# Linear attention and its feed-forward on one core: a fourth r/k slot in the decoder's scratch, r*k on another engine, and a new order

## The chip, the cores and the metric

The kernel runs on one core of one Trainium2 chip. The time is device microseconds of that core, from launch to the last instruction. A time is the median of several runs; beside them stands one profiled execution, from which every trace row here comes. PE is TensorE, DVE VectorE, ACT ScalarE, POOL GpSimd, SP the engine whose queue issues the transfers.

## The reference

Inputs are r, k, v, w of shape (4, 8, 768, 48), u of (8, 48), and two weights of (384, 2048) and (2048, 384), all float32.

```python
def _attn_ref(r, k, v, w, u):
    for t in range(S):                                   # S = 768
        cur = einsum('bhd,bhe->bhde', u[None] * k[t], v[t])
        y[t] = einsum('bhd,bhde->bhe', r[t], state + cur)
        state = w[t][..., None] * state + einsum('bhd,bhe->bhde', k[t], v[t])
    return y

def _moe_ref(x, w_in, w_out):                            # x: y as (3072, 384)
    h = x @ w_in
    g = where(h >= 1, h, where(h <= -1, 0, (h + 1)**2 / 4))
    return g @ w_out
```

## The kernel before

**Two stages in one program.** Attention goes in 12 units `u` of 256 tokens, three per batch entry. The feed-forward goes in 6 blocks `b` of 512 tokens, each made of two units, and in 16 slices `f` of the hidden width. Every feed-forward product is made of three products in a rounded format (high by high, high by low, low by high), so one step is 9 matmuls into `h` (L960) and 9 into `acc` (L980), with a gate between them: ACT L763, L764, DVE L765, ACT L767, DVE L768. Blocks 0 and 1 begin with half-width steps (`HALVES`, 5 and 11 of them for each half), so that a block can begin when its first unit is there. `h` has two PSUM banks, `g`, `gh` and `gl` three buffers each.

**A unit.** For each of two halves `q` (1 first) SP loads a `wq` tile and an `rk` tile (r and k side by side). DVE makes two scans (L439 forward, L434 backward), multiplies k (L468) and r (L518) by them; PE makes products among tokens (L488), transposes (L527), state updates (L549) and the outputs (L598); DVE picks the lower triangle (L494) and adds the states (L567 to L570). The term with u is made in two ways. In units 0 to 3 (`EARLY`) it is a scaled copy `ku` and one more set of L488. From unit 4 on a tile `nk` with r and k in another layout is loaded; POOL multiplies its halves (L506), DVE multiplies by u (L508) and sums (L511), POOL spreads the sums over `r` (L514), and DVE and PE go on. At the end ACT and DVE write `x` and `last` (L653, L655), and six small transfers (L700) fill the rest of `x`.

**Slots.** `wq` and `rk` have three slots each; a unit takes `(2u + 1 - q) % 3` of both, so one of the two tiles of the next unit waits until this unit's last matmul has read its slot.

**Weights.** They come as 64-bit words, 768 KB for each f (`wraw`, L351), at most three in flight. ACT L360 and L363, POOL L364, DVE L366, ACT L356 and DVE L369 turn them into the high and the low weight. Two scratch tiles `fl` and one `rr` hold what is between. After the decode, `fl` serves as room for 12 loads of w that a later check (L719, L720) reads.

**Unit 0** has v and a small permutation `perm` loaded in padded form (L423, L424): v into `g0` and `g1`, `perm` into a part of `nk`.

**The start of PE.** `warm` (L322) issues `SMALL` products of zeros and clears the eight banks; later, where the plan expects PE to idle for over 0.5 us, `zeros` (L335) puts products of zeros (L331) into the gap.

**The order.** Nothing is ordered by hand. `Plan.add` takes each operation with an engine, a cost, what it reads and writes, and a due time; `Plan.order` (L133) is a list scheduler that walks through modelled time and lets each free engine take, of the operations that are ready, that with the smallest key. The key is the planned time of the step that needs it, less a lead: `LEADS[u]` or `DECODES[f]` plus `SLACK` times the cost of the chain still behind it, for loads `LOADS` or `RAWS` besides. `products` into `acc` get `-LAG * AFTER` as lead, so a larger `AFTER` puts them behind other PE work. `port=True` marks operations for which DVE and POOL are modelled as sharing one port. The order that comes out is what each engine's in-order queue gets.

Of the kernel before, what the change touches and what calls it, by code (L numbers as in the profile page):

```python
# [8 lines left out]
F32 = mybir.dt.float32  # L9
# [15 lines left out]
C = 64  # L25
NC = UT // C
SEG = 2 * (UT + 1)
HP = 64
# [12 lines left out]
SMALL = 48  # L41
# [7 lines left out]
class Plan:  # L49
# [19 lines left out]
    def add(self, engine, cost, emit, due, reads=(), writes=(), port=False, size=0, fresh=True, mode=128, spare=0.0):  # L69
# [9 lines left out]
        for x in writes:  # L79
# [3 lines left out]
                             fresh=fresh and engine == "PE", touch={*reads, *writes}, mode=mode, spare=spare))  # L83
# [49 lines left out]
    def order(self):  # L133
# [10 lines left out]
        open_ = {e: [] for e in ("PE", "SP", "ACT", "DVE", "POOL")}  # L144
# [15 lines left out]
        while any(open_.values()):  # L160
# [24 lines left out]
            if op["port"]:  # L185
                port = free[e]
                first.clear()
# [31 lines left out]
SLACK = 0.759  # L219
LEADS = {0: 384.81, 1: 606.87, 2: 40.05, 3: 27.03, 4: 45.45, 5: 71.8, 6: 60.98, 7: 25.74, 8: 81.18, 9: 211.42, 10: 77.25, 11: 123.12}  # L220
DECODES = [100.35, 69.7, 39.12, 146.42, 32.88, 6.81, -6.35, -7.47, 249.78, -36.61, 27.78, -83.98, 25.56, 23.26, -16.63, -161.0]
LOADS = {0: 9.57, 1: -384.0, 2: -5.47, 3: 9.66, 4: 7.78, 5: -12.47, 6: 37.12, 7: 0.0, 8: 6.52, 9: -48.34, 10: -46.8, 11: -16.85}
RAWS = [0.0, -4.85, -25.68, 4.86, 33.83, -3.4, -2.07, 2.55, -2.88, 0.0, 79.29, 0.0, 0.0, 5.35, 18.51, -22.93]
FLIGHT = 3

EARLY = 4

GUARDED = 6

# [6 lines left out]
STEP, FIRST, PACED, AFTER = 27.1568, 703.402, 25.4941, 8.52  # L236
# [3 lines left out]
def attention_moe(tc, a):  # L240
# [46 lines left out]
    fl = tiles(2, [128, 768], F32, "fl")  # L287
    rr = one([128, 768], I32, "rr")
# [25 lines left out]
    op("POOL", 0.5, SOON, (), [("g", 2), ("s", "g2")], lambda: G.memset(g_[2][:, 0:256], 0.0))  # L314
    wide_st = {"ob0": ob[:, 0:256], "ob1": ob[:, 256:512], "g2": g_[2][:, 0:256]}
# [6 lines left out]
    def warm():  # L322
        for n in range(SMALL):
            g, h = n // 2 % 2, n % 2
            PE.matmul(bank[h][HP * g : HP * g + C, 0:C], lhsT=zero[HP * h : HP * h + HP, 0:C], rhs=zero[HP * h : HP * h + HP, 0:C],
                      start=True, stop=True)
        for b in bank:
            cleared(b, 4)
# [3 lines left out]

    op("PE", 0.16 + 0.054 * SMALL + 0.43 * 8, SOON, ["zero", "clear"], [("b", i) for i in range(8)], warm)

# [8 lines left out]
    def weight(f, when):  # L343
# [13 lines left out]

        op("SP", 0.45, due, (), [("raw", f), ("flight", f % FLIGHT)], fetch, size=786432)

# [690 lines left out]
```

## Time and profile before

| | |
|---|---|
| median of 3 runs | 505.94 us (504.72 to 509.08) |
| profiled execution | 508.8 us, its span 507.1 us |
| instructions | 13246 |
| bytes moved | 54.12 MB, mean 107 GB/s |
| HBM read, written | 46.32 MB, 4.72 MB |
| granted TensorE clock, mean | 0.998 |
| ACT busy | 296.1 us (58%) |
| POOL busy | 100.4 us (20%) |

Times in the rows further down are counted from the span's start, 1.7 us less than the device time in all. In the table of lines a group gives instructions, total, and mean; a matmul's duration reaches from its start to a modelled end and overlaps with the next, so PE's pace is read from where groups start. Products of zeros count as busy.

### The profile page before, as it was taken

Reading aid. Unit: us, or ns where it says so; the run is one execution under the profiler, and the core shown is the slowest. Engines: PE = TensorE matmul, PEld = TensorE weight load, DVE = VectorE, ACT = ScalarE, POOL = GpSimd, SP = SyncE. Lnnn points to the kernel's source line nnn. Section 1 sums busy time; section 2 is a strip of 40 time slices with the busy share of each in tenths; the row PEclk is TensorE's granted clock in tenths of the full one; section 3 lists DMA queues with packets and bytes.
Section 4 is the critical chain, followed back from the end, with each engine's and each line's share of the span. In section 5 each row is a group of like instructions: output and inputs, shape, how many; then the busy total and the mean of one; then the engine's idle time right before and its main releaser. Section 6 shows DMA issues by size and latency. Waiting matters only on the chain.

```text
span 507.1 us, 13246 instructions
## 1 busy us (share of the span) xinstructions
PE 492.8 (97%) x5562; PEld 412.5 (81%) x5562; DVE 332.2 (66%) x560; ACT 296.1 (58%) x605; POOL 100.4 (20%) x68
## 2 busy tenths in 40 slices
PE   8999999999999999999999899999999999999995
PEld 6778987889999988888878678888887888888884
DVE  6899997956998699849555979842364333243331
ACT  3597798987875564745643565653454444454441
POOL 2487766801012321102001112100010000000000
PEclk9999999999999999999999999999999999999999
DMA  8984734326643434505006342300110000100001
GB/s 297 403 296 147 281 145 153 126 64 208 201 126 97 140 108 143 167 11 204 23 1 193 106 134 90 123 1 1 63 49 13 17 1 0 63 2 0 1 1 67
DMA packets 21922, 54.12 MB, mean 107 GB/s; under 512 B 3104, under 2 KB 8672, under 8 KB 21856
## 3 DMA queue, kind: packets, MB, share of 16 engines
q1 hardware_dynamic: 21856, 53.21, 31.5%
q8 instruction: 45, 0.74, 0.6%
q14 instruction: 21, 0.17, 0.1%
HBM read 46.32 MB, written 4.72 MB: 101 GB/s over the span
## 4 chain that ended last, share of the span: by engine, by line
PE 75%; DVE 13%; DMA 4%; ACT 3%; issue 3%; SPq 1%; ACTq 0%; DVEq 0%
PE h L960 33%; PE acc L980 33%; PE bank L598 4%; DVE y L434 2%; DVE gl L768 2%; PE bank L488 2%; DMA rk<-in_rk 2%; DVE p L439 1%; DMA wraw<-in_wbits 1%; DVE wt L369 1%; PE bank L527 1%; PE bank L549 1%; DVE r L494 1%; DMA wq<-in_w 1%; DVE g L765 1%
## 5 line engine op out<-in xcount | busy, mean ns | idle before, releaser
L960 PE MATMUL h<-x,wt 128*128 128x512 f32 (+1 forms) x1008 | 216.8, 361 | 1.9 <-DVE g L765 1.3
L960 PEld LDWEIGHTS h<-x,wt 128*128 128x128 f32 x1008 | 168.3, 188 | 31.8 <-DVE g L765 1.9
L980 PE MATMUL acc<-gh,wt 128*128 128x512 f32 (+1 forms) x672 | 152.2, 360 | 0.0
L980 PEld LDWEIGHTS acc<-gh,wt 128*128 128x128 f32 x672 | 113.8, 188 | 19.0
L765 DVE SCALAR_TENSOR_TENSOR g<-g,h 128x512 f32<-128x512 f32 (+1 forms) x112 | 67.4, 605 | 92.1 <-ACT g L764 84.9
L763 ACT ACTIVATE g<-h 128x512 f32<-128x512 f32 (+1 forms) x112 | 59.7, 533 | 85.8 <-PE h L960 84.1
L768 DVE TENSOR_TENSOR gl<-g,gh 128x512 fp32r<-128x512 f32 (+1 forms) x112 | 73.3, 659 | 28.9 <-ACT gh L767 13.5
L767 ACT CAST gh<-g 128x512 fp32r<-128x512 f32 (+1 forms) x112 | 62.1, 558 | 39.6 <-PE acc L980 18.6
L980 PE MATMUL acc<-gl,wt 128*128 128x512 f32 (+1 forms) x336 | 84.5, 357 | 0.1
L980 PEld LDWEIGHTS acc<-gl,wt 128*128 128x128 f32 x336 | 58.4, 187 | 10.0 <-DVE gl L768 0.5
L764 ACT ACTIVATE g<-g 128x512 f32<-128x512 f32 (+1 forms) x112 | 64.0, 571 | 3.3
L364 POOL TENSOR_SCALAR rr<-wraw 128x768 uint16<-128x768 f32 x16 | 52.7, 3291 | 35.0 <-DVE fl L366 17.3
L514 POOL TENSOR_TENSOR r<-cst,d 128x512 f32<-128x512 f32 x16 | 17.3, 1104 | 157.0 <-PE bank L598 131.9
L506 POOL TENSOR_TENSOR nk<-nk 128x768 f32<-128x768 f32 x8 | 16.8, 2096 | 83.7 <-DMA nk<-in_nk 74.5
L439 DVE TENSOR_TENSOR_SCAN p<-wq,seeds 128x514 f32<-128x514 f32 x24 | 30.2, 1259 | 3.7 <-DMA wq<-in_w 2.8
L434 DVE TENSOR_TENSOR_SCAN y<-wq,seeds 128x514 f32<-128x514 f32 x24 | 30.8, 1282 | 0.8
L468 DVE TENSOR_TENSOR rk<-rk,y 128x512 f32<-128x512 f32 x24 | 18.9, 789 | 3.1 <-DMA rk<-in_rk 2.9
L331 PE MATMUL bank<-clear 128*128 128x512 f32 (+1 forms) x57 | 17.1, 418 | 1.8 <-DVE seeds L438 1.8
L369 DVE TENSOR_TENSOR wt<-fl,wt 128x768 fp32r<-128x768 f32 x16 | 16.5, 1033 | 3.2 <-ACT wt L356 3.1
L598 PEld LDWEIGHTS bank<-rk,st 48*48 48x48 f32 (+1 forms) x656 | 11.4, 121 | 8.6 <-DVE st L567 2.9
L363 ACT ACTIVATE rr<-wraw 128x768 uint16<-128x768 uint32 x16 | 17.5, 1094 | 1.1 <-DVE fl L366 1.1
L518 DVE TENSOR_TENSOR rk<-rk,p 128x512 f32<-128x512 f32 x24 | 17.7, 749 | 0.2 <-PE acc L488 0.2
(108 smaller groups left out, 384.5 us busy)
## 6 DMA issues: line engine op xcount, KB each, us to landing
rk<-in_rk SPq DMA_DIRECT2D x24, 512.0 KB, 4.8
wraw<-in_wbits SPq DMA_DIRECT2D x16, 768.0 KB, 7.9
wq<-in_w SPq DMA_DIRECT2D x24, 257.5 KB, 3.3
nk<-in_nk SPq DMA_DIRECT2D x8, 768.0 KB, 4.8
vn<-in_v SPq DMA_DIRECT2D x11, 384.0 KB, 5.8
fl<-in_w SPq DMA_DIRECT2D x12, 257.0 KB, 2.9
out_y<-g SPq DMA_DIRECT2D x11, 256.0 KB, 2.3
x<-last SPq DMA_DIRECT2D x66, 32.0 KB, 2.5
```

Of the source, the lines that this page charges most:

```text
L364: op("POOL", 3.35, due, [("raw", f)], ["rr_high"], lambda: G.tensor_scalar(out=r16[:, :, 1], in0=wraw[f][:, :, 1].bitcast(F32), scalar1=0. ...
L369: op("DVE", 0.95, due, [("fl", k), ("wh", f)], [("wl", f)], lambda: V.tensor_tensor(out=w_lo[f], in0=s, in1=w_hi[f].bitcast(F32), op=ALU.s ...
L434: V.tensor_tensor_scan(out=y_[:, ::-1], data0=w[:, SEG:0:-1], data1=sv[:, ::-1], initial=0.0, op0=ALU.mult, op1=ALU.add)
L439: V.tensor_tensor_scan(out=pv[:, q].rearrange("p n c -> p (n c)"), data0=w[:, 0:SEG], data1=sv, initial=0.0, op0=ALU.mult, op1=ALU.add,)
L598: PE.matmul(out=bank[by[g]][HP * half : HP * half + wide, lo : lo + C], start=first, stop=False, skip_group_check=True, **kw)
L763: op("ACT", c, due, [("b", 6 + hk)], [("g", gk)], lambda: nc.scalar.activation(gs, hs, AF.Relu, scale=0.5, bias=0.5))
L764: op("ACT", c, due, (), [("g", gk)], lambda: nc.scalar.activation(gs, gs, AF.Square))
L765: op("DVE", 0.13 + 0.56 * k, due, [("b", 6 + hk)], [("g", gk)], lambda: nc.vector.scalar_tensor_tensor(out=gs, in0=gs, scalar=1.0, in1=hs, ...
L767: op("ACT", c, due, [("g", gk)], [("gh", gk)], lambda: nc.scalar.copy(ghs, gs))
L768: op("DVE", 0.18 + 0.52 * k, due, [("g", gk), ("gh", gk)], [("gl", gk)], lambda: nc.vector.tensor_tensor(out=gls, in0=gs, in1=ghs.bitcast( ...
L960: nc.tensor.matmul(by16(hp, f), lhsT=wx[f][:, cs], rhs=by16(xt[:, j, :], f), start=n == 0, stop=n == 8)
L980: nc.tensor.matmul(by16(o[j]), lhsT=wx[f][:, cs], rhs=by16(gt), start=first and i == 0, stop=stop and i == 2, skip_group_check=True)
```

## The change

- `fl`, `rr` and three new uses share one tile `scratch`: two `fl` and `rr` as before, then, when all weights are decoded, a fourth slot of `rk` (columns 0 to 1023) and two `stage` tiles (1024 to 1535 and 1536 to 2047).
- From unit 4 on (`FOUR`) a unit takes the slots `u % 2` and `u % 2 + 2` of `rk`; `wq` keeps three. Loads into slot 3 wait for all 16 decodes.
- Block outputs with j = 1 and 2 go out through `stage`, no longer through `g1` and `g2` (except in the last block), and the check's loads of w go to `stage`, without the column that isn't needed.
- r*k in `nk` (L506) moves from POOL to DVE.
- Unit 0 takes v as the other units do and ACT spreads it into `g0` and `g1`, cleared by POOL; `perm` is made on POOL from the identity. Three loads become one.
- `warm` makes 12 products of 256 columns where it made 48 of 64.
- The plan: new leads, `SLACK` 2.283 for 0.759, `AFTER` 122.415 for 8.52; loads are planned to land 1 us later than before (`MARGIN`); POOL's L364, L450 and L514 now stand in the model as holding the port for 0.8, 0.27 and 0.93 us.

```diff
-SMALL = 48
+SMALL = 12
...
             if op["port"]:
-                port = free[e]
+                port = free[e] if op["hold"] is None else t + op["hold"]
...
-SLACK = 0.759
-LEADS = {0: 384.81, 1: 606.87, 2: 40.05, 3: 27.03, 4: 45.45, 5: 71.8, 6: 60.98, 7: 25.74, 8: 81.18, 9: 211.42, 10: 77.25, 11: 123.12}
-DECODES = [100.35, 69.7, 39.12, 146.42, 32.88, 6.81, -6.35, -7.47, 249.78, -36.61, 27.78, -83.98, 25.56, 23.26, -16.63, -161.0]
+SLACK = 2.283
+LEADS = {0: 313.28, 1: 332.14, 2: 30.3, 3: -35.92, 4: 59.61, 5: 8.14, 6: 58.69, 7: -189.33, 8: -17.53, 9: 10.22, 10: -177.85, 11: 56.6}
+DECODES = [151.83, 107.97, 105.43, 231.96, 14.9, -48.19, 3.2, 263.77, 168.2, 7.46, 92.06, 298.21, 156.44, 134.24, 312.98, 121.85]
...
+MARGIN = 1.0
+FOUR = 4
...
-STEP, FIRST, PACED, AFTER = 27.1568, 703.402, 25.4941, 8.52
+STEP, FIRST, PACED, AFTER = 27.1568, 703.402, 25.4941, 122.415
...
-    fl = tiles(2, [128, 768], F32, "fl")
-    rr = one([128, 768], I32, "rr")
+    scratch = one([128, 3 * 768], F32, "scratch")
+    fl = [scratch[:, 0:768], scratch[:, 768:1536]]
+    rr = scratch[:, 1536:2304].bitcast(I32)
+    rk = [*rk, scratch[:, 0:1024].rearrange("p (a c) -> p a c", a=2)]
+    stage = [scratch[:, 1024:1536], scratch[:, 1536:2048]]
+    decoded = [("wl", f) for f in range(NF)]
...
-            PE.matmul(bank[h][HP * g : HP * g + C, 0:C], lhsT=zero[HP * h : HP * h + HP, 0:C], rhs=zero[HP * h : HP * h + HP, 0:C],
-                      start=True, stop=True)
+            PE.matmul(bank[h][HP * g : HP * g + C, 0 : 4 * C], lhsT=zero[HP * h : HP * h + HP, 0:C],
+                      rhs=zero[HP * h : HP * h + HP, 0:C].unsqueeze(1).broadcast_to([HP, 4, C]), start=True, stop=True)
...
-        slot = [(2 * u + 1 - q) % 3 for q in range(2)]
+        wslot = [(2 * u + 1 - q) % 3 for q in range(2)]
+        slot = wslot if u < FOUR else [u % 2, u % 2 + 2]
+        behind = [] if u < FOUR else decoded
...
+            load(due, rk[slot[q]], a["rk"][u, q], [("k", slot[q]), ("r", slot[q])], behind if slot[q] == 3 else [], spare=MARGIN if u > 1 else 0.0)
...
         if alone:
+            load(due, v[:, :, 0:DM], a["v"][u], [("v", 0)])
             for c2 in range(2):
-                load(due, g_[c2], a["v0"][c2], [("g", c2)])
-            load(due, perm, a["perm"], ["perm", "nk"])
+                op("ACT", 0.48, due, [("v", 0)], [("g", c2)], lambda c2=c2: A.copy(
+                    g_[c2].rearrange("p (h e) -> p h e", e=HP)[:, :, 0:D], v[:, c2, 0:DM].rearrange("p (h e) -> p h e", e=D)))
+            op("POOL", 0.4, due, (), ["perm", "nk"], lambda: G.memset(perm, 0.0))
+            op("POOL", 0.3, due, ["cst"], ["perm"], lambda: G.tensor_copy(
...
-            op("POOL", 2.2, due, (), ["nk"], lambda: G.tensor_tensor(
+            op("DVE", 0.94, due, (), ["nk"], lambda: V.tensor_tensor(
                 out=nk[:, :, 0, :], in0=nk[:, :, 0, :], in1=nk[:, :, 1, :], op=ALU.mult), port=True)
...
-            o, ok = (ob, "ob") if j == 0 else (g_[m], ("g", m))
+            o, ok = (ob, "ob") if j == 0 else (g_[m], ("g", m)) if done else (stage[j - 1], ("stage", j - 1))
```

## Rows read from the trace of the kernel before

**Rows 1.** The page: busy time, share, instructions; then tenths in 40 slices.
```profile
PE 492.8 (97%) x5562; PEld 412.5 (81%) x5562; DVE 332.2 (66%) x560; ACT 296.1 (58%) x605; POOL 100.4 (20%) x68
...
PE   8999999999999999999999899999999999999995
PEld 6778987889999988888878678888887888888884
DVE  6899997956998699849555979842364333243331
```

**Rows 2.** Busy time by stage: window, length, engines' busy us, granted clock, DMA share, GB/s.
```profile
9.50:27.50 18.00, 16.58 (x363) 13.12 (x361) 14.94 (x25) 10.11 (x21) 7.62 (x3) 1.00 1.03 405
27.50:57.30 29.80, 27.89 (x588) 24.50 (x586) 29.43 (x48) 24.00 (x51) 24.56 (x11) 1.00 0.62 208
57.30:84.00 26.70, 25.50 (x215) 22.07 (x219) 26.25 (x42) 24.51 (x42) 16.48 (x6) 1.00 0.49 187
...
118.00:300.00 182.00, 179.40 (x2385) 154.00 (x2379) 142.06 (x254) 109.46 (x258) 27.13 (x19) 1.00 0.39 124
```

**Rows 3.** The same windows, zeros alone (L331): PE busy, PEld busy, clock, DMA, GB/s.
```profile
9.50:27.50 18.00, 8.74 (x32) 5.22 (x31) 1.00 1.03 405
27.50:57.30 29.80, 4.29 (x16) 2.46 (x15) 1.00 0.62 208
57.30:84.00 26.70, 0.00 (x0) 0.00 (x0) 1.00 0.49 187
```

**Rows 4.** Waits of PE from 118 to 300 us: engine, line, releaser, total, times, longest.
```profile
PE bank L488 <- DVE seeds L438: 1.3, 1, 1.3
PE h L960 <- DVE g L765: 0.5, 1, 0.5
PE bank L598 <- DVE st L567: 0.5, 1, 0.5
```

**Rows 5.** Timeline 275 to 293 us: start, length, instruction, idle before and releaser.
```profile
276.19 0.69 DVE L468 TENSOR_TENSOR rk<-rk,y 128x512 f32<-128x512 f32 x1 [2.16 <-DMA rk<-in_rk]
...
279.19 2.03 POOL L506 TENSOR_TENSOR nk<-nk 128x768 f32<-128x768 f32 x1 [9.31 <-DMA nk<-in_nk]
279.47 2.30 DVE L518 TENSOR_TENSOR rk<-rk,p 128x512 f32<-128x512 f32 x1
...
281.82 1.16 PE L488 MATMUL bank<-rk 64*64 64x64 f32 x64 [1.28 <-DVE seeds L438]
...
292.13 0.67 PE L598 MATMUL bank<-rk,st 48*48 48x64 f32 x32 [0.53 <-DVE st L567]
```

**Rows 6.** Timeline 150 to 160 us, the same columns.
```profile
155.31 2.42 DVE L768 TENSOR_TENSOR gl<-g,gh 128x256 fp32r<-128x256 f32 x2
155.60 1.85 POOL L506 TENSOR_TENSOR nk<-nk 128x768 f32<-128x768 f32 x1 [2.57 <-DMA nk<-in_nk]
...
158.73 1.33 PE L960 MATMUL h<-x,wt 128*128 128x256 f32 x9 [0.55 <-DVE g L765]
```

**Rows 7.** Single lines: count, duration ns min/median/max, first and last start, form.
```profile
L506 POOL TENSOR_TENSOR nk<-nk x8: 1834/1853/2812, 123.7 to 307.8; 128x768 f32<-128x768 f32 x8
L508 DVE TENSOR_TENSOR nk<-nk,u_sb x8: 932/949/957, 136.7 to 312.4; 128x768 f32<-128x768 f32 x8
L518 DVE TENSOR_TENSOR rk<-rk,p x24: 665/684/2299, 11.3 to 380.0; 128x512 f32<-128x512 f32 x24
L364 POOL TENSOR_SCALAR rr<-wraw x16: 3069/3168/4090, 17.1 to 99.4; 128x768 uint16<-128x768 f32 x16
L434 DVE TENSOR_TENSOR_SCAN y<-wq,seeds x24: 1227/1228/1950, 5.4 to 329.9; 128x514 f32<-128x514 f32 x24
```

**Rows 8.** POOL's and SP's waits for `nk` and slots; landing of `nk`, issue to landing.
```profile
POOL nk L506 <- DMA nk<-in_nk: 74.5, 7, 21.2
...
SPq L301 <- PE bank L598: 105.4, 13, 24.4
...
DMA to landing us min/median/max: 4.1/4.7/6.3
```

**Rows 9.** DVE's timeline in unit 0's chain, 11 to 28 us.
```profile
12.25 1.23 DVE L439 TENSOR_TENSOR_SCAN p<-wq,seeds 128x514 f32<-128x514 f32 x1 [0.30 <-DMA wq<-in_w]
...
14.86 0.67 DVE L518 TENSOR_TENSOR rk<-rk,p 128x512 f32<-128x512 f32 x1
...
25.00 0.96 DVE L366 SCALAR_TENSOR_TENSOR fl<-fl,rr 128x768 int32<-128x768 int32 x1 [1.33 <-POOL rr L364]
```

**Rows 10.** PE's timeline: the small zeros, and the end of PE's first wait.
```profile
2.94 2.84 PE L325 MATMUL bank<-zero 64*64 64x64 f32 x96
...
9.49 0.60 PE L527 MATMUL bank<-cst,rk 128*128 128x128 f32 x4
```

## What was predicted

> **What bounds the kernel now.** I read the page first, then the windows by stage, then what ended PE's idle time, then the timelines around those places. The page says that PE is busy for 97% of the span and that no other engine comes near [rows 1]. That figure counts products of zeros, so the windows have to be read with the zeros beside them. From 9.5 to 84 us PE lost three pieces: length less busy time plus zeros is 18.00 - 16.58 + 8.74 = 10.2 us, then 29.80 - 27.89 + 4.29 = 6.2 us, then 26.70 - 25.50 = 1.2 us, together 17.6 us [rows 2, 3]. In the same three windows DVE was idle for only 3.06 + 0.37 + 0.45 = 3.9 us of 74.5. So this stage, in which four units of attention and sixteen weight decodes meet, belongs to DVE. From 118 to 300 us PE lost 182.00 - 179.40 = 2.6 us, and 2.3 us of them are three waits for DVE [rows 2, 4]. There DVE itself has 182.00 - 142.06 = 39.9 us free. After that the tenths of PE stand at 9 to the last slice [rows 1]: a pure PE stage, whose work the change leaves alone.
>
> So there are two places to win in: 2.3 us in the middle, up to 17.6 us in the start. The matmuls of the two layers and of attention are the same before and after.
>
> **The change part by part.** The sum is made against the profiled execution, 508.8 us, of which 507.1 are span and 1.7 lie around it; the median of the runs is 505.94, 2.9 us lower, and a gain is taken to be the same on both.
>
> *r*k on DVE.* It removes eight POOL instructions of 1.85 us and adds eight on DVE; the nearest row is L508, same tile and shape, 0.95 us, so 8 x 0.95 = 7.6 us of DVE in a stage that has 39.9 free [rows 2, 7]. What it gives back is larger than the step itself. At 279.19 L506 runs on POOL, and a DVE product with two SBUF inputs that began 0.28 us later took 2.30 us where the line's median is 0.68; PE then waited 1.28 us [rows 5, 7]. At 155.60 the same happens: two L768 take 2.42 us together, and PE waits 0.55 us [rows 6]. The sum of these two waits is 1.8 us, and both go with L506. Bounds: nothing, if POOL's other product in that stage (L514) falls on the same DVE work instead, and the whole 2.3 us. I take 1.8.
>
> The Trainium skill, SBUF — State Buffer, section "SBUF: two separate sides", says that DVE and GpSimd share one pair of ports under an exclusive lock that the first to start keeps for its whole instruction. The 1.6 us by which L518 grew agree with it. By the same rule the moved product can itself be held up by L514, which stays on POOL, and each L364 would hold such DVE work for its 3.2 us; the longest backward scan, at 1.95 us against 1.23, shows only 0.72 us added [rows 7], so for L364 the measurement decides. By that rule taken whole, the moved product would keep some of the collisions and the 1.8 would shrink towards nothing; by the rows it stays.
>
> *The wait that moves with it.* POOL spent 74.5 us waiting for `nk` to land, at no cost, because nothing urgent stood behind [rows 8]. Now that wait stands in DVE's in-order queue, and behind it are the gates (L765, L768) that PE needs. The transfer takes 4.7 us from issue to landing and 6.3 at worst, a spread of 1.6 us [rows 8]. The plan has 1 us of margin on it, and PE carries up to two steps of `acc` products as cover. I price it at nothing; without the cover it is up to 1.6 us in each of 8 units, 12.8 us. It is the rival on the slower side.
>
> *The fourth slot.* SP waited 13 times and 105.4 us in all for the matmul that frees a slot [rows 8]. In one place this reached PE: L468 waited 2.16 us for `rk` at 276.19, DVE then had three scans and the triangles in a heap, and PE waited another 0.53 us at 292.13 [rows 5]. With four slots a unit's tiles can be loaded a whole unit earlier. This gives 0.5 us, bounds 0 and 0.5 beside the term above. Slots 3 and `stage` are aliases of decode scratch; every use comes after the last decode, and the last L364 starts at 99.4 us [rows 7], before unit 5 needs a slot. Outputs through `stage` take the out-transfers off `g1` and `g2`; no row of PE's waits shows such a stall [rows 4], so nothing.
>
> *Twelve wide zeros.* The same columns in a quarter of the instructions. The 48 took 2.84 us from 2.94 us on, and PE's first real work comes at 9.49 us [rows 10], after more zeros. Hidden by that wait, either way. The granted clock is 1.00 in the windows from 9.5 us on [rows 2], and nothing says that the wide ones keep PE less busy. Nothing.
>
> *Unit 0 without three loads, and the new order, taken together.* Both act on the stage of 9.5 to 84 us. `v` and `perm` are 320 KB less in all; at the 405 GB/s of that window [rows 2] the first weights land 0.8 us earlier, and two copies of about half a microsecond go to an ACT that is idle for 7.9 of 18 us. The order: unit 0's second L518 (14.86) stands behind a scan pair of unit 1 that began at 12.25 [rows 9], so its chain could be 2.6 us shorter. Bounds: at best PE gets back the 6.2 + 1.2 us of the later windows and 2.6 + 0.8 of the first, 10.8 us. At worst the order puts a unit's four scans (4 x 1.23 = 4.9 us) in front of something that PE waits for. The nearest row for a middle value is DVE's own idle time: if the same DVE work has to be done in this stage, 3.9 us is all that can be won, and about 0.9 of it are gaps of a hop that no order closes. I take 3.0. What speaks for a gain at all: the decodes get leads of mostly over 100 us, the products into `acc` become PE's last choice and so a reserve, and unit 3, whose output is needed only in block 1's second half, gets a lead of -36 us in place of 27.
>
> Sum: 1.8 + 0.5 + 3.0 = 5.3 us; 508.8 - 5.3 = 503.5 as a profiled execution, 505.94 - 5.3 = 500.6 us as a median.
>
> **The rivals.** *The start stays as it is.* DVE is busy for 95% of 9.5 to 84 us whatever the order, and a weight's decode passes five times between engines. Then only the middle is won: 505.94 - 2.3 = 503.6 us. For it speaks that the DVE work of the stage is unchanged; against it that PE's lost 17.6 us are over four times DVE's idle 3.9, so part of it is choice.
>
> *The change does not reach PE.* The new loads are asked for no earlier than before, since the plan places them by due times, and the moved product meets L514 instead of L506. Then it is 505.9 us. For it: PE idled for 2.6 of 182 us in the middle anyway. Against: the two stalls lie exactly under L506.
>
> *DVE stands in line for `nk`.* One mechanism: the moved product waits at the head of DVE's queue. Place: units 4 to 11. Price: up to 1.6 us uncovered in each. It decides when the units lose more on average than the 5.3 us won plus 5.1 (1%), that is 10.4 / 8 = 1.3 us each, which needs PE's reserve of `acc` products to be empty each time. At that point the time is 511 us, at full price 505.94 - 5.3 + 12.8 = 513.4 us.
>
> **How the numbers follow.** A measurement of this kernel can tell about 1% (5 us) from no change. My forecast, the gain in both places, has 0.46: around 500.6, its own range 495.6 to 503 (the lower end is 505.94 - 2.3 - 8, most of the 10.8). The start unchanged has 0.32, no reach 0.10, the wait for `nk` or another misordering with more cost than gain 0.12. Faster by over 1% is below 500.9 us, where I put the larger part of the forecast and of luck in the start: 0.46. Within 1%: 0.41, from the second and third case and the upper part of the first. Slower by over 1%: 0.13. The range leaves out most of the slower case and the best end of the start: 495.5 to 508.5, where 508.5 is 505.94 + 4.9 - 2.3.
>
> **What would show it.** In the trace after: no POOL instruction of `nk` and no DVE product of two SBUF inputs above 1 us outside L514 and L364; PE's waits between 118 and 300 us below 1 us in all; the first L960 before 27 us; zeros from 9.5 to 57 us below 13.0 us; PE's waits naming neither `nk` nor the new product. The forecast is wrong if zeros and idle time before 84 us stay near 17 us, if L768 or L765 wait for the DMA of `nk`, or if PE goes idle at the start of a block.

## The result and the profile after

The changed kernel takes 501.59 us (median of 4 runs, 500.79 to 503.27); the kernel before, on the same chip, took 506.16 (4 runs, 504.72 to 509.08). The ratio is 0.9896, with a 95% interval of 0.9867 to 0.9926: 4.6 us gained where 5.3 were forecast. A second set of runs (after_again below) gives 0.9866 and 6.9 us, so the forecast lies between the two. Its profiled execution took 503.27 us, of which 501.6 are span. The lines have moved: zeros L331 is L341, the weight's decode L364, L366 and L369 is L374, L376 and L379, the scans L434 and L439 are L451 and L456, the two loads' products L468 and L518 are L485 and L535, r*k L506 is L523, L488 is L505, L598 is L615, the gates L765 and L768 are L782 and L785, and the feed-forward products L960 and L980 are L977 and L997.

The page's busy times answer [rows 1]. r*k's eight products have left POOL, which is busy for 16.5 us less; DVE has eight instructions more and is nevertheless busy for 5.2 us less.

```profile
PE 491.2 (98%) x5488; PEld 412.4 (82%) x5488; DVE 327.0 (65%) x568; ACT 298.1 (59%) x607; POOL 83.9 (17%) x64
```

The stages of [rows 2], the same columns: window, length, busy time and count of PE, PEld, DVE, ACT and POOL, granted clock, DMA share, GB/s.

```profile
9.50:27.50 18.00, 15.30 (x342) 12.67 (x332) 12.87 (x22) 9.08 (x19) 7.96 (x3) 0.91 0.99 376
27.50:57.30 29.80, 29.03 (x580) 25.50 (x582) 28.02 (x49) 24.83 (x53) 21.43 (x11) 1.00 0.56 201
57.30:84.00 26.70, 26.70 (x367) 23.59 (x360) 25.74 (x44) 26.11 (x51) 18.25 (x8) 1.00 0.57 213
118.00:300.00 182.00, 182.00 (x2553) 157.04 (x2552) 147.06 (x278) 103.39 (x243) 16.20 (x14) 1.00 0.36 116
```

The zeros alone (L341) in the first two, as in [rows 3]; the third window again has none.

```profile
9.50:27.50 18.00, 7.53 (x26) 5.04 (x27) 0.91 0.99 376
27.50:57.30 29.80, 6.76 (x24) 3.55 (x22) 1.00 0.56 201
```

The middle is as forecast: from 118 to 300 us PE idles for 0 us, where it was 2.6. The start is not: length less busy time plus zeros is 10.2 + 7.5 + 0 = 17.8 us, against 17.6 before. PE's timeline also has the first feed-forward product later, at 31.18 us; before it came at 27.46. The kernel before, then the changed one:

```profile
27.46 1.22 PE L960 MATMUL h<-x,wt 128*128 128x256 f32 x6
...
31.18 2.04 PE L977 MATMUL h<-x,wt 128*128 128x256 f32 x15
```

Yet the start did give something, and counting PE's matmuls shows it. First the kernel before from 0 to 84 and 84 to 300 us, all engines, then L960, L980, L331 and the outputs L598 alone up to 84 us (PE and PEld):

```profile
0.00:84.00 84.00, 77.68 (x1275) 65.90 (x1279) 76.27 (x122) 62.20 (x120) 51.65 (x38) 1.00 0.69 250
84.00:300.00 216.00, 213.40 (x2705) 181.91 (x2702) 163.65 (x284) 137.98 (x308) 41.75 (x25) 1.00 0.39 122
...
0.00:84.00 84.00, 21.64 (x126) 17.88 (x126) 1.00 0.69 250
...
0.00:84.00 84.00, 18.89 (x117) 16.30 (x117) 1.00 0.69 250
...
0.00:84.00 84.00, 18.03 (x62) 11.10 (x62) 1.00 0.69 250
...
0.00:84.00 84.00, 4.79 (x248) 4.24 (x252) 1.00 0.69 250
```

Then the changed kernel, in a second profiled execution (the first experiment below): the same two stretches, then L977, L997, L341 and the outputs L615 up to 84 us.

```profile
0.00:84.00 84.00, 78.59 (x1321) 66.00 (x1321) 74.16 (x124) 63.82 (x129) 52.87 (x44) 1.00 0.70 254
84.00:300.00 216.00, 216.00 (x2827) 185.42 (x2826) 180.95 (x326) 128.27 (x285) 29.34 (x19) 1.00 0.36 118
...
0.00:84.00 84.00, 23.67 (x135) 19.40 (x135) 1.00 0.70 254
...
0.00:84.00 84.00, 16.22 (x108) 14.55 (x108) 1.00 0.70 254
...
0.00:84.00 84.00, 18.19 (x60) 11.05 (x60) 1.00 0.70 254
...
0.00:84.00 84.00, 7.12 (x368) 6.13 (x368) 1.00 0.70 254
```

At 84 us both have done 243 feed-forward products (126 + 117 and 135 + 108). Of the rest, the kernel before had 1275 - 243 - 62 - 96 (its small zeros) = 874 matmuls of attention, the changed one 1321 - 243 - 60 - 24 = 994. So 120 more matmuls of attention lie behind it at the same moment, in nearly the same "lost" time (16.9 us in this second execution). All 120 are outputs, 368 - 248, and take 7.12 - 4.79 = 2.3 us. What stands after 84 us agrees in size: 507.1 - 84 = 423.1 us before, 500.8 - 84 = 416.8 after, 6.3 less. Of these, 2.6 are the idle time removed; 0.5 are a shorter end behind PE's last matmul, which ends at 501.74 us before and at 495.91 after; the other 3.2 are work already done at 84 us. The "lost" time does not show this gain, and since a matmul's end is modelled, PE's busy time does not price it.

### The profile page after: what moved, and what is told of

Same layout as the page of the kernel before. It is cut to its first block, busy times and chain, and to the rows that moved or that the text cites. A ratio compares the mean times of both kernels' runs of the same rounds, so it can differ in the third digit from the quotient of the medians.

```text
span 501.6 us, 13003 instructions
## 1 busy us (share of the span) xinstructions
PE 491.2 (98%) x5488; PEld 412.4 (82%) x5488; DVE 327.0 (65%) x568; ACT 298.1 (59%) x607; POOL 83.9 (17%) x64
## 4 chain that ended last, share of the span: by engine, by line
PE 91%; DVE 2%; issue 0%; ACT 0%; ACTq 0%; DVEq 0%
PE acc L997 40%; PE h L977 40%; PE bank L615 5%; PE bank L505 3%; PE bank L544 2%; PE bank L566 2%; DVE r L511 0%; DVE scratch L376 0%; DVE wt L379 0%; PE bank L341 0%; DVE p L456 0%; DVE rk L535 0%; DVE st L584 0%; DVE rk L485 0%; PE bank L681 0%
## 5 line engine op out<-in xcount | busy, mean ns | idle before, releaser
L977 PE MATMUL h<-x,wt 128*128 128x512 f32 (+1 forms) x1008 | 215.2, 360 | 0.0
L977 PEld LDWEIGHTS h<-x,wt 128*128 128x128 f32 x1008 | 169.2, 187 | 29.2
L997 PE MATMUL acc<-gh,wt 128*128 128x512 f32 (+1 forms) x672 | 153.2, 361 | 0.0
L997 PEld LDWEIGHTS acc<-gh,wt 128*128 128x128 f32 x672 | 113.3, 188 | 18.7
L785 DVE TENSOR_TENSOR gl<-g,gh 128x512 fp32r<-128x512 f32 (+1 forms) x112 | 67.7, 609 | 71.6 <-PE acc L997 56.9
L782 DVE SCALAR_TENSOR_TENSOR g<-g,h 128x512 f32<-128x512 f32 (+1 forms) x112 | 67.7, 606 | 63.8 <-ACT g L781 63.5
L997 PE MATMUL acc<-gl,wt 128*128 128x512 f32 (+1 forms) x336 | 84.3, 356 | 0.0
L997 PEld LDWEIGHTS acc<-gl,wt 128*128 128x128 f32 x336 | 58.5, 187 | 9.5
L531 POOL TENSOR_TENSOR r<-cst,d 128x512 f32<-128x512 f32 x16 | 18.3, 1164 | 253.6 <-PE bank L615 215.0
L374 POOL TENSOR_SCALAR scratch<-wraw 128x768 uint16<-128x768 f32 x16 | 51.2, 3198 | 34.7 <-DVE scratch L376 27.1
L456 DVE TENSOR_TENSOR_SCAN p<-wq,seeds 128x514 f32<-128x514 f32 x24 | 29.7, 1238 | 2.7 <-DMA wq<-in_w 1.8
L451 DVE TENSOR_TENSOR_SCAN y<-wq,seeds 128x514 f32<-128x514 f32 x24 | 30.1, 1256 | 0.8
L373 ACT ACTIVATE scratch<-wraw 128x768 uint16<-128x768 uint32 x16 | 17.6, 1100 | 3.0 <-DVE scratch L376 1.5
L551 ACT COPY kt<-bank 128x512 f32<-128x512 f32 x24 | 13.7, 583 | 8.4 <-PE bank L544 8.1
L376 DVE SCALAR_TENSOR_TENSOR scratch<-scratch 128x768 int32<-128x768 int32 x16 | 15.7, 981 | 2.2 <-ACT scratch L373 2.1
L341 PE MATMUL bank<-clear 128*128 128x512 f32 (+1 forms) x48 | 14.9, 430 | 2.1 <-DVE seeds L455 2.1
L379 DVE TENSOR_TENSOR wt<-scratch,wt 128x768 fp32r<-128x768 f32 x16 | 15.3, 963 | 1.7 <-ACT wt L366 1.6
L370 ACT ACTIVATE scratch<-wraw 128x768 f32<-128x768 f32 x16 | 15.0, 940 | 2.1 <-DVE wt L379 1.1
L511 DVE COPY_PREDICATED r<-below,bank 128x512 f32<-128x512 int32 x22 | 15.2, 736 | 1.4 <-PE bank L505 1.3
```

The costliest lines, as they stand in the source:

```text
L374: op("POOL", 3.15, due, [("raw", f)], ["rr_high"], lambda: G.tensor_scalar(out=r16[:, :, 1], in0=wraw[f][:, :, 1].bitcast(F32), scalar1=0. ...
L451: V.tensor_tensor_scan(out=y_[:, ::-1], data0=w[:, SEG:0:-1], data1=sv[:, ::-1], initial=0.0, op0=ALU.mult, op1=ALU.add)
L456: V.tensor_tensor_scan(out=pv[:, q].rearrange("p n c -> p (n c)"), data0=w[:, 0:SEG], data1=sv, initial=0.0, op0=ALU.mult, op1=ALU.add,)
L531: op("POOL", 1.07, due, ["d", "cst"], [("R", h)], lambda h=h: G.tensor_tensor(out=r_[h], in0=twice.unsqueeze(1).unsqueeze(1).broadcast_to( ...
L782: op("DVE", 0.13 + 0.56 * k, due, [("b", 6 + hk)], [("g", gk)], lambda: nc.vector.scalar_tensor_tensor(out=gs, in0=gs, scalar=1.0, in1=hs, ...
L785: op("DVE", 0.18 + 0.52 * k, due, [("g", gk), ("gh", gk)], [("gl", gk)], lambda: nc.vector.tensor_tensor(out=gls, in0=gs, in1=ghs.bitcast( ...
```

## Experiments

Each ratio is to the kernel before in runs on the same chip, with its 95% interval. "The stretch" is my sum over DVE's instructions of duration less the median of the same line and shape, where it is over 0.05 us. It is given by what the instruction's own row shows, up to 84 us and after 118 us: 4.3 and 8.3 us in the kernel before.

**The changed kernel once more** (after_again; code unchanged, to have a second trace beside the others).

> The changed kernel once more, beside the runs below. It should repeat the ratio 0.990 (0.987 to 0.993). In the first profile PE stood still for 1.82 us at 20.97 us with nothing named that it waited for, and the granted clock was half of full for 3.4 us soon after. Theory A: this is part of the new order in the start, and it comes again at the same place, 1 us or more. Theory B: it is an accident of one execution; then the stall is below 0.5 us here and the first L977 starts at about 29 us in place of 31.2.

501.18 us, ratio 0.9866 (0.9843 to 0.9889). PE's pause came again at the same place, 1.21 us long, as theory A has it (last section). The stretch is 1.7 and 0.7 us; in the first profile it was 0.7 and 0.7. This is the mark that the edits of the changed kernel are held against.

**r*k alone moved, everything else as before** (before_rk_dve).

```diff
-            op("POOL", 2.2, due, (), ["nk"], lambda: G.tensor_tensor(
+            op("POOL", 2.2, due, (), ["nk"], lambda: V.tensor_tensor(
```

> The kernel before with one word changed: L506 runs on DVE; the order of everything is that of the kernel before. Theory A (the port): the PE waits of 1.28 us at 281.8 and 0.55 us at 158.7 go, 1.8 us faster, ratio 0.996. Theory B (DVE's queue): the product's place was chosen for POOL, so DVE stands in line for the transfer of nk and PE loses as much as it wins or more: ratio 1.000 to 1.02, with gates waiting for the DMA of nk in the rows. Theory C: DVE's stretched instructions were not on PE's path: 1.000, and the two PE waits stay.

506.37 us, ratio 0.9963 (0.9947 to 0.9980), so 1.9 us of 508.09. PE's waits from 118 to 300 us, total, times, longest, are down from the three of [rows 4] to

```profile
PE bank L598 <- DVE st L567: 0.5, 1, 0.5
PE bank L527 <- DVE r L494: 0.2, 1, 0.2
```

and the stretch after 118 us falls from 8.3 to 2.5 us, while up to 84 us it stays at 4.3, since L506 does not run there. PE's idle time from 118 to 300 us falls from 2.60 to 0.76 us, by 1.8. The first term of the sum is measured, as theory A has it: 1.9 us (1.0 to 2.7) for 1.8.

**The converse: r*k back on POOL in the changed kernel, order kept** (after_rk_pool).

```diff
-            op("DVE", 0.94, due, (), ["nk"], lambda: V.tensor_tensor(
+            op("DVE", 0.94, due, (), ["nk"], lambda: G.tensor_tensor(
```

> The changed kernel with one word changed back: r*k (L523) runs on POOL; the order of everything stays the new one. Theory A (the port): DVE products with two SBUF inputs that meet it grow from 0.7 to about 2.3 us and some of that reaches PE: 1 to 2 us slower than the changed kernel, ratio to the kernel before 0.993 to 0.995. Theory B (the reserve): in the new order PE has products into acc left whenever DVE is late, so the same stretched instructions cost nothing: ratio 0.990 and no PE wait above 0.3 us after 84 us.

504.52 us, ratio 0.9938 (0.9916 to 0.9959): 3.3 us slower than the changed kernel, where the old order gives 1.9. The new order puts the first units' r*k among the last decodes, where DVE has little to spare: from 84 to 118 us it is busy for 33.7 of 34 us in the changed kernel, where it was 21.6 before. DVE's groups from 84 to 118 us (line, form, count, busy us, mean ns, idle before), this kernel first, then the changed kernel in its second profile:

```profile
L376 DVE SCALAR_TENSOR_TENSOR scratch<-scratch 128x768 int32<-128x768 int32 x5 | 6.4, 1278 | 0.0
...
L456 DVE TENSOR_TENSOR_SCAN p<-wq,seeds 128x514 f32<-128x514 f32 x3 | 5.2, 1728 | 0.1
```

```profile
L376 DVE SCALAR_TENSOR_TENSOR scratch<-scratch 128x768 int32<-128x768 int32 x5 | 4.8, 950 | 0.0
L456 DVE TENSOR_TENSOR_SCAN p<-wq,seeds 128x514 f32<-128x514 f32 x3 | 3.9, 1297 | 0.1
```

These two lines are 2.9 us longer, and it is two instructions, each beside an L523 on POOL. The first of them in the timeline, POOL and DVE:

```profile
102.98 2.17 POOL L523 TENSOR_TENSOR nk<-nk 128x768 f32<-128x768 f32 x1
...
103.38 2.58 DVE L376 SCALAR_TENSOR_TENSOR scratch<-scratch 128x768 int32<-128x768 int32 x1
```

L376 takes 2.58 us where its median is 0.95. After 118 us two gates L785 are stretched as well, by 0.7 and 1.6 us. The order being the same, each matmul of PE can be set against itself in the changed kernel's second profile: it starts 0.7 us earlier at the first feed-forward product, 0.8 us later at 123 us and 2.0 us later from 221 us on. So both stretches reach PE. That part of the change is confirmed in both directions; with 1.0 to 2.7 us for the 1.9, and more than 1 us of uncertainty in each of the two ratios behind the 3.3, that its size depends on the order is likely and not shown.

**The new code in the old order** (new_code_old_order and new_code_old_order2). In the changed kernel the instructions are sorted by the times that the plan of the kernel before gave each; in the second, the check on w and its loads have the new plan's times.

```diff
-        for emit in plan.kept_warm(plan.best(step_ops, dues), "PE", [("b", i) for i in range(8)], zeros):
+        for emit in plan.kept_warm(forced(plan, BEGIN, END), "PE", [("b", i) for i in range(8)], zeros):
...
```

> All new code (fourth slot, stage, r*k on DVE, unit 0 without three loads, 12 wide zeros), but every instruction in the place that the plan of the kernel before gave it; the few new ones stand where the loads that they replace stood. Theory A (as predicted): the code alone wins the middle, 1.8 + 0.5 us, and some of the start: ratio 0.994 to 0.996. Theory B (the order is all): ratio 0.999 to 1.001, idle time of PE from 118 to 300 us still over 2 us. Theory C (the code is all): 0.990.

> New code in the old order once more, with one mend: the check's loads of w and the check itself stand where the new order has them, since through the shared stage tile they cannot come before the block outputs, and in the first try DVE and PE stood in line for them for 50 us. Theory A (as predicted): the middle is won, ratio 0.994 to 0.996. Theory B (the order is all): 0.999 to 1.001; up to 330 us the first try had made as many feed-forward products as the kernel before and no more, which speaks for B. Theory C (the code is all): 0.987 to 0.990.

The first took 561.2 us (ratio 1.1046, 1.1015 to 1.1076), nearly all through one wait:

```profile
PE bank L847 <- DVE above L744: 49.8, 1, 49.8
```

The kernel's check on w loads into `stage`, the tiles that the block outputs now use too, and in the old order its product stands on PE before the outputs have let go of them. That says only that `stage` has to be planned for, so in the second kernel the check has its new place. It took 507.35 us, ratio 0.9988 (0.9974 to 1.0001): nothing that can be told from noise, and by its middle value less than r*k alone gave in the same order, though the two intervals just overlap. PE's two longest waits from 118 to 300 us, and a pause in PE's timeline:

```profile
PE bank L544 <- DVE r L511: 0.7, 1, 0.7
PE bank L615 <- DVE st L584: 0.5, 1, 0.5
...
22.95 0.57 PE L615 MATMUL acc<-r,g 64*64 64x64 f32 x22 [1.27 <-issue]
```

The first feed-forward product starts 1.0 us later than in the kernel before, at 28.46 us, behind this pause, which the kernel before does not have. Set against the same matmuls there, PE then wins 2.2 us between 158 and 283 us, where r*k's two stalls were, and ends 0.9 us ahead. So in these two executions r*k's gain is there and the start takes part of it back. The 0.5 us wait for `st` (L615, before L598), from which the prediction drew the fourth slot's term, is still there: in the old order a fourth slot brings nothing that can be measured.

**The old code in the new order** (old_code_new_order): the same sorting with the plans exchanged, loads asked for as soon as their slot's release allows.

> All old code (three slots, r*k on POOL, outputs through g1 and g2, three loads for unit 0, 48 small zeros) in the new order; what depends on a slot or buffer that the old code does not have is issued as soon as its release has been issued. Theory A (two parts that add): the start's gain comes, the middle's does not, ratio 0.993 to 0.996. Theory B (the order needs the code): loads that the new order asks for early now stand in SP's queue for a slot and everything behind them waits: 1.01 or more. Theory C (the order is all): 0.987 to 0.990.

641.41 us, ratio 1.2629 (1.2607 to 1.2652). Its waits (engine, line, releaser, total, times, longest):

```profile
PE h L960 <- DVE g L765: 77.7, 22, 8.2
...
DVE rk L468 <- DMA rk<-in_rk: 45.0, 8, 8.5
```

**The changed kernel with three slots, order kept** (after_three_slots): no unit gets the fourth slot.

```diff
-FOUR = 4
+FOUR = 12
```

> The changed kernel with the fourth slot of r and k taken away and all else kept, the order too; a load that now has to wait for a slot is issued as soon as the slot's last reader has been issued. Theory A (as predicted): worth about 0.5 us, ratio 0.987 to 0.990. Theory B: the new order leans on the early loads, so units start late and PE runs out of other work: 5 us slower or more, ratio 0.997 to 1.01, with waits of DVE for the DMA of rk. Theory C: no difference at all.

563.2 us, ratio 1.1101 (1.1087 to 1.1115), some 62 us slower than with four. (The instructions are sorted by the changed kernel's own planned times.) PE's, DVE's and SP's waits:

```profile
PE h L977 <- DVE g L782: 43.3, 8, 8.1
DVE rk L485 <- DMA rk<-in_rk: 42.7, 8, 8.5
...
SPq L309 <- PE bank L615: 90.6, 11, 21.1
```

SP can't ask for `rk` before L615 has freed a slot, L485 waits at the head of DVE's queue for the load, and the gate L782 that PE needs stands behind it. This is the mechanism that the prediction feared for `nk`, on another tile: 43 of the 62 us in 8 waits. So the new order leans on the slot. What a plan searched afresh for three slots would give was not tried; the nearest thing to it is the kernel before.

**The small zeros back** (after_small48): 48 products of 64 columns, as in the kernel before, instead of 12 of 256; same order.

```diff
-        for n in range(SMALL):
+        for n in range(48):
...
-            PE.matmul(bank[h][HP * g : HP * g + C, 0 : 4 * C], lhsT=zero[HP * h : HP * h + HP, 0:C],
-                      rhs=zero[HP * h : HP * h + HP, 0:C].unsqueeze(1).broadcast_to([HP, 4, C]), start=True, stop=True)
+            PE.matmul(bank[h][HP * g : HP * g + C, 0:C], lhsT=zero[HP * h : HP * h + HP, 0:C], rhs=zero[HP * h : HP * h + HP, 0:C],
+                      start=True, stop=True)
```

> The changed kernel with 48 products of zeros of 64 columns at the start in place of 12 of 256; the order is the same. Both theories: within 0.5 us of the changed kernel (ratio 0.986 to 0.991), since PE waits at that point. What it tells apart besides: the stall of PE of 1.2 to 1.8 us near 21 us, for which the trace names nothing, came in three profiles of the new order. Theory A: it goes with the number of instructions issued before it; with 72 more records it moves to another place or goes. Theory B: it goes with the work at that place, and stays at the same matmul (L615).

501.34 us, ratio 0.9878 (0.9864 to 0.9892): the same as the changed kernel within the intervals. In the profiled execution something did move. PE's pause near 21 us is gone, as theory A has it (last section), and from 38 to 280 us PE's matmuls start some 1.4 us earlier than the same ones in the changed kernel's second profile. Then the lead falls to 0.4 us. DVE's and PE's timeline there:

```profile
278.22 0.96 DVE L523 TENSOR_TENSOR nk<-nk 128x768 f32<-128x768 f32 x1 [1.79 <-DMA nk<-in_nk]
...
279.83 2.30 PE L977 MATMUL h<-x,wt 128*128 128x512 f32 x9 [0.47 <-DVE g L782]
```

SP had asked for this `nk` at 271.03 us, 7.2 us before DVE could begin; in the second profile of the changed kernel it was 5.5 us. DVE stands in line for the load, the gate L782 behind it is late, and PE gives back 1.0 us of its lead. So a slow load hides in this profile what the start had gained; how it went in the other runs of this kernel is not shown.

**L364 cut short, in both kernels** (before_short_pool and after_short_pool). POOL's step of the decode runs over 8 of the 768 columns, so that 3.17 us become 0.27; the signs of the weights in the other columns are left out. POOL clears `rr` once at the start instead (not shown in the edit). The times of planning stay. The edit in the kernel before:

```diff
-            out=r16[:, :, 1], in0=wraw[f][:, :, 1].bitcast(F32), scalar1=0.0, scalar2=32768.0, op0=ALU.is_lt, op1=ALU.mult))
+            out=r16[:, 0:8, 1], in0=wraw[f][:, 0:8, 1].bitcast(F32), scalar1=0.0, scalar2=32768.0, op0=ALU.is_lt, op1=ALU.mult))
```

> The kernel before, its order kept, with POOL's part of a weight's decode (L364) cut from 768 to 8 columns: the signs of all other columns of the weights are left out, so POOL holds the port it shares with DVE for next to nothing and its 3.2 us are gone from each decode. In the first 84 us DVE's instructions took 4.3 us longer than the median of their own lines, nearly all under L364 and L450. Theory A (the port in the start): this is what the start lost: 2 to 4 us faster, ratio 0.992 to 0.996, DVE's excess below 1 us before 84 us. Theory B (the order of operations itself): the stretched instructions were covered, ratio 0.998 to 1.000 although the excess is gone.

> The changed kernel, its order kept, with the same cut (signs of all but 8 columns of the weights left out). DVE's excess in its first 84 us was 0.7 to 1.7 us. Theory A (the new order already keeps DVE and POOL apart, and that is its gain): little left to win, within 1 us of the changed kernel, ratio 0.986 to 0.990. Theory B (the gain has another source): the cut wins as much here as in the kernel before.

In the old order 505.26 us, ratio 0.9936 (0.9919 to 0.9953), 3.1 us of 508.39. In the new order 501.09 us, ratio 0.9854 (0.9837 to 0.9871), which overlaps the changed kernel's own interval. The short L364 does two things: it takes POOL out of DVE's way, and it shortens the chain of each decode by 2.9 us, for which DVE had stood in line once in the old order, 1.33 us at 25.00 [rows 9]. The first is seen in DVE's groups up to 84 us: the kernel before, then the same with L364 cut short.

```profile
L369 DVE TENSOR_TENSOR wt<-fl,wt 128x768 fp32r<-128x768 f32 x11 | 11.7, 1069 | 0.9 <-ACT wt L356 0.9
L434 DVE TENSOR_TENSOR_SCAN y<-wq,seeds 128x514 f32<-128x514 f32 x8 | 11.1, 1389 | 0.3
```

```profile
L369 DVE TENSOR_TENSOR wt<-fl,wt 128x768 fp32r<-128x768 f32 x11 | 10.6, 970 | 0.9 <-ACT wt L356 0.9
L434 DVE TENSOR_TENSOR_SCAN y<-wq,seeds 128x514 f32<-128x514 f32 x8 | 9.9, 1240 | 0.3
```

The same instructions, 2.3 us shorter in two lines; the whole stretch up to 84 us falls from 4.3 to 0.3. Which of the two PE gained from is seen by setting the same matmuls side by side, the kernel before and then with L364 cut short:

```profile
57.31 2.39 PE L960 MATMUL h<-x,wt 128*128 128x256 f32 x18 [0.24 <-DVE g L765]
83.86 0.67 PE L598 MATMUL bank<-rk,st 48*48 48x64 f32 x32 [0.84 <-DVE st L567]
```

```profile
57.36 2.39 PE L960 MATMUL h<-x,wt 128*128 128x256 f32 x18
82.38 0.67 PE L598 MATMUL bank<-rk,st 48*48 48x64 f32 x32
...
156.55 1.22 PE L960 MATMUL h<-x,wt 128*128 128x256 f32 x9
```

The first feed-forward product starts 0.3 us later there (27.79 us for 27.46), so up to 57 us the shorter chain can have given PE some 0.3 us. Between 57 and 84 us PE gains 1.5 us. PE's only waits there are 1.4 us for DVE in the kernel before; DVE waits nowhere for L364, and four of its instructions lose 1.8 us beside it. So in the old order it is the collisions that cost. Another 0.7 us comes by 158.73 [rows 6], where in the kernel before two gates L768 met L506 and in this execution none does; that is luck of the shift. The same comparison of the two profiles in the new order gives 0.6 us by 19 us and 0.2 more by 23 us, and nothing after that: the 0.65 us that one scan still loses at 81 us does not reach PE there.

**The changed kernel, planned without the short hold** (after_plan_no_hold). The change tells the planner that L374 and L467 (L364 and L450 before) hold the port for 0.8 and 0.27 us. Here they hold nothing and are costed as before, and the order is searched anew with the new leads. L531 (L514 before) keeps its 0.93 us.

```diff
-        op("POOL", 3.15, due, [("raw", f)], ["rr_high"], lambda: G.tensor_scalar(
+        op("POOL", 3.35, due, [("raw", f)], ["rr_high"], lambda: G.tensor_scalar(
-            out=r16[:, :, 1], in0=wraw[f][:, :, 1].bitcast(F32), scalar1=0.0, scalar2=32768.0, op0=ALU.is_lt, op1=ALU.mult), port=True, hold=0.8)
+            out=r16[:, :, 1], in0=wraw[f][:, :, 1].bitcast(F32), scalar1=0.0, scalar2=32768.0, op0=ALU.is_lt, op1=ALU.mult))
-                    op("POOL", 2.7, due, [("k", s), "cst"], [("ku", q), "nk"], lambda q=q: with_u(q), port=True, hold=0.27)
+                    op("POOL", 2.6, due, [("k", s), "cst"], [("ku", q), "nk"], lambda q=q: with_u(q))
```

> The changed kernel, planned anew with one thing changed in the model: L374 and L467 on POOL do not count as holding the port (as in the plan of the kernel before), their costs as there. All leads stay. Theory A (the port): DVE's excess before 84 us is back at about 4 us and 2 to 3 us are lost, ratio 0.992 to 0.995. Theory B: the leads carry the order, the excess stays below 2 us: within 1 us of the changed kernel. A ratio above 1.0 says only that the leads suit no other model.

506.6 us, ratio 0.9969 (0.9958 to 0.9979). Against the changed kernel's 0.9866 that is 1.0%, some 5 us where theory A had 2 to 3: most of the gain is gone, with the slot, the leads and r*k on DVE all still there. The stretch up to 84 us is back at 3.5 us. The stage of 57.3 to 84 us, which PE had filled, and one of PE's waits over the whole span:

```profile
57.30:84.00 26.70, 24.82 (x321) 21.11 (x320) 26.42 (x43) 24.03 (x47) 17.61 (x7) 1.00 0.59 207
...
PE h L977 <- DVE g L782: 2.3, 3, 1.4
```

**The old `AFTER`** (after_after8): 122.415 back to 8.52, replanned, to test whether products into `acc` held back as a reserve carry the start.

> The changed kernel, planned anew with AFTER at 8.52 in place of 122.415: products into acc are no longer PE's last choice. Theory A (the reserve, as I put it in the prediction): PE has less left over when DVE is late, 1 to 4 us slower than the changed kernel, ratio 0.990 to 0.996, with PE waiting for L782 in the rows. Theory B: no part of the gain: 0.986 to 0.989.

559.83 us, ratio 1.0998 (1.0962 to 1.1033). PE's longest group of waits is for `x<-last`, 8.7 us in 6 waits, and the zeros (L341), which the planner lays into gaps that it foresees, take 62 us where the changed kernel has 18. The new leads don't fit the old value, so the plan is a bad one in its own right. Inconclusive: whether the reserve helps stays open.

## Why the prediction was right, and where it was not

**r*k on DVE: right, and measured.** 1.8 us forecast, 1.9 measured in the order in which it was costed. In the new order it is worth 3.3 by its middle value, which the prediction's rows could not show. The place is right too: PE's waits from 118 to 300 us are gone. DVE's stretch after 118 us, 8.3 us before, is 0.7; the move alone takes it to 2.5.

**The wait for `nk`: right in the changed kernel, with little room.** It is in DVE's queue now and costs nothing there. L523's row and its wait, in the changed kernel:

```profile
L523 DVE TENSOR_TENSOR nk<-nk x8: 931/956/1326, 102.0 to 279.3; 128x768 f32<-128x768 f32 x8
...
DVE nk L523 <- DMA nk<-in_nk: 1.0, 2, 0.6
```

Two waits of 0.6 us at most, and PE waits for none of them. The rival on the slower side would have needed 1.3 us in each of eight units. That the mechanism exists is shown by after_three_slots, and on `nk` itself by after_small48: one wait of 1.79 us, over the 1.6 that the prediction took as the spread, and PE lost 1.0 us behind it.

**The fourth slot: wrong as a term.** It was put into the sum as 0.5 us that come by themselves. In the runs the parts do not add: new code in the old order 0.9988, the new order without the slot 1.1101, both together 0.9866. The step that failed is treating a tile and the order that uses it as separate items; the 0.5 can't be told from nothing.

**Twelve wide zeros: the total right, the reason not.** The prediction had them hidden by PE's first wait. The time is the same either way within the intervals, but a pause near 21 us comes with them, and in the profile without it PE was 1.4 us ahead until a slow load took most of that back. So the step is not as free of effects as it was priced, and that the profiles end alike is luck.

**The start: the size about right, the reason wrong.** 3.0 us were forecast, from DVE's 3.9 us of idle time, a shorter chain for unit 0 and a reserve of products. By the prediction's own tests this falls: the first feed-forward product should have come before 27 us and came at 31.18, zeros from 9.5 to 57 us should have been below 13.0 us and are 7.5 + 6.8 = 14.3, and zeros and idle time stayed near 17 us, which it had named as proof against itself. What was won instead is 3.2 us of work done by 84 us (above); that 3.0 came near it is luck. DVE's idle time was the wrong bound: from 9.5 to 84 us it did not shrink but grew, from 3.9 to 74.5 - 12.87 - 28.02 - 25.74 = 7.9 us. DVE's *busy* time shrank, from 70.6 to 66.6 us: the prediction took its length as given ("the same DVE work"), and it was not.

In the kernel before all 4.3 us of stretch up to 84 us lie in ten DVE instructions, and each of the ten ran beside an L364 (seven, 3.6 us) or an L450 (three, 0.7 us). The timeline of before, POOL and DVE, shows the worst, the scan that the prediction had seen in [rows 7] and set aside as "only 0.72 us":

```profile
74.82 3.11 POOL L364 TENSOR_SCALAR rr<-wraw 128x768 uint16<-128x768 f32 x1 [1.61 <-DVE seeds L433]
...
74.85 1.95 DVE L434 TENSOR_TENSOR_SCAN y<-wq,seeds 128x514 f32<-128x514 f32 x1
```

POOL began 0.03 us earlier, and the scan grew by 0.72 us. The prediction read the row rightly as one collision, and did not count how many there are in the stage that DVE sets. The change's 0.8 us for L364 stood in the diff and was passed over. That is the failed step. Three runs bear the new reason out: cutting L364 short gives the old order 3.1 us, of which the matmuls set side by side put some 1.5 on the collisions up to 84 us, and the new one 0.6 (0.9866 to 0.9854, inside the intervals), and planning without the hold brings the stretch back and costs 5 us. How much of the start's 3.2 us is due to it, and how much to the rest of the order, these runs do not separate.

**What the whole comes to.** The changed kernel gains 1.04% in the first set of runs and 1.34% (1 - 0.9866) in the second. r*k alone gives 0.37% and L364 cut short 0.64%, each in the old order, and part of the 0.64% is the luck named above; since the parts do not add across orders, these are no shares of the whole. What the new order and the slot add together is not shown to have one cause. after_plan_no_hold is a plan of its own, so its 5 us hold some luck of the search beside the stretch; unit 0's three missing loads were not tried alone, nor were the leads.

## What to carry to other kernels

When an in-order engine sets a stage, its busy time is not a given: compare each of its instructions with the median of its line, add up what exceeds it, and look what ran on the engine that shares its port. A short collision is worth modelling in a planner; here collisions of 0.7 us at most, beside a step of the decode, cost PE some 1.5 us in the old order, nearly what moving the instruction with the longest hold gave. Where two runs have the same order, set the same matmul of both side by side: the place where its start moves tells which wait was paid for, where busy and idle time do not. A tile and the order that uses it are to be tested crosswise, old and new of each, since either alone can be worth nothing or cost 60 us.

## What the runs showed of the hardware

**Two POOL operations, two holds.** L506, a product of two tiles, delayed L518 by 1.6 us [rows 5, 7]: L518 ended at 281.77, and less its median of 0.68 that is 281.09, within 0.13 us of L506's end at 281.22. L523 on POOL did the same to L376 (above): 103.38 + 2.58 - 0.95 = 105.01, within 0.14 us of L523's end at 105.15. L364, a comparison with scalars over 3.1 us, delayed DVE by 0.72 at most. In all seven collisions up to 84 us in the kernel before, the moment at which a DVE instruction of median length must have begun lies 2.33 to 2.36 us before L364's end; the scan shown at 74.85 gives 74.85 + 0.72 = 75.57, which is 0.75 after L364's start and 2.36 before its end at 77.93. The Trainium skill, SBUF — State Buffer, section "SBUF: two separate sides", has the port pair held for the whole instruction. The trace agrees for L506 and differs for L364, whose hold is a quarter of its length; there the measurement decides. The prediction had seen that difference and missed that 0.7 us is still a price.

**PE's own pause.** In dense runs of small products PE stopped once for nothing that the profile shows ("issue"). PE's timeline of the changed kernel:

```profile
20.11 0.86 PE L615 MATMUL acc<-r,g 64*64 64x64 f32 x43
22.80 0.50 PE L615 MATMUL acc<-r,g 64*64 64x64 f32 x17 [1.82 <-issue]
```

and of the kernel with 48 small zeros in place of 12 wide ones:

```profile
20.40 1.11 PE L615 MATMUL acc<-r,g 64*64 64x64 f32 x60
```

It came again after the same 43 products in the second profile of the changed kernel, at 1.21 us, and is absent where 72 more instructions went before. All nine profiles of kernels with the 12 wide zeros have it, 0.63 to 1.82 us long at L615; none of the five with 48 small ones has. The two kernels take the same time, 501.34 and 501.18 us, but in the profile without the pause PE is ahead up to the wait for `nk` (above), and with the new code in the old order the first feed-forward product comes 1.0 us later behind it. So that it costs nothing is not shown, and neither is what it is.

**The clock once.** In the first profile of the changed kernel PE was granted 0.50, the lower level of 1.2 GHz, right after that pause of 1.82 us (window, length, busy time of the engines, granted clock):

```profile
23.60:26.90 3.30, 3.30 (x14) 3.01 (x13) 0.96 (x1) 2.18 (x4) 1.40 (x2) 0.50 0.90 335
```

After the pause of 1.21 us in the second profile it stayed at 1.00. In after_after8 it fell to 0.50 at 239.6 us, after idle times of PE of 0.42 and 1.20 us close together, so the length of one pause does not settle it. The two executions of the changed kernel took 503.27 and 502.33 us.
